# Attention with chunk selection and a gated FFN: eleven SBUF copies as transfers of SyncE, twenty-three loads on Pool's queue, and a new order table

## The chip, the cores and the metric

One core of a Trainium2 chip. The metric is the device time of one execution in microseconds (us). The engines are called as in the profile: PE (TensorE), DVE (VectorE), ACT (ScalarE), POOL (GpSimd) and SP (SyncE, which here issues transfers only). A name such as SPq is the DMA queue that an engine issues into.

## The reference

```python
# q, k, v: (4 batches, 8 heads, 768 tokens, 64), float32
k_min, k_max = k_chunks.min(3), k_chunks.max(3)              # 24 chunks of 32 keys
ub = sum(maximum(q*k_min, q*k_max), -1)                       # a bound per query and chunk
ub = where(causal, ub, -1e9)
top_chunks = argsort(ub)[..., -6:]                            # six chunks for each query
scores = where(selected & causal, q @ k.T / 8, -1e9)
attn_out = softmax(scores) @ v
x = attn_out as (3072 tokens, 512)
out = (sigmoid(x @ w_gate) * (x @ w_val)) @ w_out             # 512 -> 1536 -> 512
```

So each query looks only at the keys of the six chunks with the largest bound, and at none behind itself. All of it is computed by one program.

## The kernel before, in words

*Tiles.* The 24 blocks of 128 tokens are done in eight units u0 to u7 of three blocks, that is 384 columns. u0 takes the first blocks of batches 0, 1 and 2, u1 the blocks 1 to 3 of batch 0, u2 the last two of batch 0 and the first of batch 3, u3 and u4 those of batch 1 with the first free one of batch 2, and so on to u7, the last three of batch 3. A unit's keys and queries are loaded, turned (k and q so that head dimension lies on partitions), their chunk minima and maxima taken (kx), the bounds formed on PE (ub), the six largest chosen (mx), and a mask row per chunk written into the rows that the scores' product reads beside q (ap, apt, hqm). The keys' side holds the turned keys (hk) and the constant pattern of the chunks (hkp).

*Attention.* For each pair of heads PE forms the scores (sc), ACT the exponential (exp), Pool the causal cut where it is needed (cm), PE the product with v (pv), DVE the division (rz, x), and PE turns x back (xps, xT). The first blocks of the batches (u0) run the same steps under names that end in f: vf (load of v), scf, expf, pvf, rzf, xf, xpsf, xTf.

*FFN.* For every unit there are products g and v (gate and value, four matmuls of 128 x 384 each), ACT's tanh, DVE's hg (gate times value) and the product o with w_out, then osb and out. u0 to u3 run this plainly. u4 with u5 and u6 with u7 are done in pairs, by a scheme of seven products for eight (function `ffn_pair`).

*Names.* A number behind the name is the head, pair or half, then the unit or the batch: hk0_2_2 is the even half of batch 2's turned keys for pair 2, hqm1_u5_0 the mask row of u5, k11_2 a quarter of batch 2's k. Batches 1 to 3 load k and q in four transfers each, in runs of 128 bytes; u1 and u2 load theirs by pairs (k0_u1 to q3_u2); v comes by block of 128 tokens (v_2_3), all by SP's queue. The weights wg0 to wo2 come by Pool's queue, converted on the way. Of k, q and v each buffer is used again later, so that a load may have to wait for the last reader of what stood there.

*The order.* All work is entered into a `Plan` with its engines, its reads and its writes. It is then emitted in the order of a long string, `ORDER`, of 1,893 names, written out ahead. In it `name:3` gives the buffer's slot and `name@ACT` an engine other than the first one listed for that operation. Each engine, and each queue, works through its own share of the string in order, so one instruction that waits holds up all behind it on its engine; for a load that waits for its buffer, that is everything behind it on SP.

```python
for op in plan.order():
    op.emit(op.engine)
```

The functions that the change touches, with the lines that the profile names:

Of the kernel before, what the change touches and what calls it, by code (L numbers as in the profile page):

```python
# [94 lines left out]
tri0 ap1 ident epat0:0 ident16 tri k2_u1:0 kn_u1_2:0 kT_u1_2:0 kt_u1_2:0 q1_u2:1 vf1_1:1 epat kcr0 kx0_u1_2  # L95
qn_u2_1@DVE:2 k1_u2 k3_u1 kf1_0:0 q0_u1 qn_u1_0@DVE:3 qT_u1_0:1 qf_u1_0@DVE:0 kx1_u1_2:0 k1_u1 kn_u1_3:4 hkp001@ACT
kT_u1_3:2 q2_u2 hkp010@ACT qf0_0:1 qn_u2_2:5 hkp100@ACT q2_u1 qT_u2_1:3 scm_0:4,5 hkp101@POOL kn_u1_1@POOL:6 kT_u1_1:6
kt_u1_3:1 kx0_u1_3 kx1_u1_1 hq0 hkp000 k0_u1 kn_u1_0@POOL:0 kT_u1_0:7 kt_u1_0@DVE:2 q1_u1 qn_u1_1@POOL:3 qf0_1:2
hq1_u1_0 qf_u2_1:1 hq0_u2_1@POOL qT_u1_1:0 qf1_0 kf0_0 qf_u1_1@DVE q3_u1 kf1_2:3 kfT_0:1 kf16_0@DVE:4 hk0_u1_3@ACT
hk1_u1_3@ACT kx1_u1_3 kx0_u1_1 qfT_0:3 qn_u1_2:2 qf16_0:6 kt_u1_1:1 hk0_u1_2@POOL hkp110@POOL qT_u2_2:0 qn_u1_3@POOL:0  # L100
qT_u1_3:2 qf_u1_3 kn_u2_1:3 vf_1:4 vc_1 qT_u1_2:3 hkf1 hk1_u1_1@POOL hkf0@DVE kx0_u1_0 qm_u1_1:0 kx1_u1_0 kf0_2 qf1_1
kf1_1:5 kfT_2:6 kf0_1 qf0_3:0 qf_u1_2 qm_u1_3@ACT hk0_u1_1@ACT qf1_2:1 qf0_2 hk0_u1_0@POOL vf_2:4 qf_u2_2 vf_0:3 kfT_1:2
kxf1:1 scf_0:1 kf16_2:5 expf_0_0 qfT_1:3 kf16_1@DVE:0 kcr1 kxf0 hkp011 qfT_2:7 scm_1:0,2 qm_u1_0@POOL qf16_1:2 scf_1:2
qm_u1_2@ACT kcr_u1@POOL v10 qf16_2:4 v16_0_0 expf_1_1:3 expf_1_0 hkp111@ACT q3_u2 kcr_f ub_u1:6,4 ubn0_u1:0 ubm0_u1
kf1_3:5 ubn1_u1 k2_u2 qf1_3 pvf_1_1:1 pvf_0_0:3 kT_u2_1:7 mx0_u1:0 pvf_1_0:2 ap0_u1 qfT_3:0 rzf_0_0:0 k0_u2 wg0
hq1_u1_2@POOL wv0 apt0_u1:0 rzf_1_1:1 xf_0_0:0 hk1_u1_0@ACT kn_u2_2:6 qf16_3:0 hq0_u1_1 expf_0_1:1 kT_u2_2:6 kx0_u2_2
hq0_u1_0@POOL vf1_2:2 k3_u2 hq0_u1_2@POOL scm_2:4,0 scf_2:2 expf_2_1:0 hqm0_u1_0 vc_2 xpsf_0_0:5,0 xf_1_1:1 rzf_1_0:0
pvf_0_1:3 rzf_0_1:1 qn_u2_3@POOL:3 xf_1_0:2 q0_u2 sc_u1_0_1:0,1 hqm0_u1_2 expf_2_0 vf1_3:1 xpsf_1_1:1 xTf_1_1 pvf_2_0:4
qn_u2_0:6 xTf_0_0@ACT xpsf_1_0:2 rzf_2_0:0 xTf_1_0 xf_2_0:0 qT_u2_0:5 qf_u2_0@DVE kt_u2_2@DVE:1 kx1_u2_1:0
kn_u2_0@POOL:4 hq0_u1_3@POOL hq1_u1_3@POOL kt_u2_1@DVE:2 hk1_u1_2@POOL qm_u2_1@ACT:0 exp_u1_0_1 sc_u1_1_2:1,3 xpsf_2_0:4  # L110
exp_u1_1_2 xTf_2_0@ACT qT_u2_3:0 qf_u2_3 sc_u1_1_0:2 pvf_2_1:1 rzf_2_1:0 sc_u1_0_0:5 exp_u1_1_0 sc_u1_2_2:4,2 xf_2_1:1
hk1_u2_2@POOL exp_u1_2_2 xf_0_1:2 sc_u1_3_1:0,0 exp_u1_3_1 sc_u1_3_2:2 sc_u1_2_0:4 xpsf_2_1:1 sc_u1_3_0:0 exp_u1_0_0
exp_u1_3_0 v_0_2:2 kf0_3 hk0_u2_2@ACT xTf_2_1 qm_u2_2 ubm1_u1 kx1_u2_2 kn_u2_3@POOL:5 hk0_u2_1@POOL v16_0_2 xpsf_0_1:3
kT_u2_3:5 v_0_3:1 v_0_1:3 wg1 xTf_0_1 sc_u1_0_2:1 ap0 kT_u2_0:0 sc_u1_2_1:6 sc_u1_1_1:3 exp_u1_2_0 exp_u1_1_1 kx0_u2_1
wv1 cm_u1_1 v16_0_1 kx0_u2_0 v16_0_3 exp_u1_2_1 g_u0_0:4,0,0 exp_u1_0_2 tanh_u0_0 kfT_3:7 v_u0_0:3 mx1_u1 kx0_u2_3
ap1_u1 apt1_u1 exp_u1_3_2 kf16_3:6 kt_u2_3@DVE:0 g_u0_1:6,1,1 qm_u2_0@ACT tanh_u0_1 v_u0_1:1 vf_3:0 g_u0_2:4,2,2
v_u0_2:2 hqm1_u1_0@ACT qm_u2_3@ACT hq1_u1_1 pv_u1_1:7 kx1_u2_3 cm_u1_0 pv_u1_0 tanh_u0_2 hq1 sc_u1_4_1:5,3 k11_1:0
hqm1_u1_2 cm_u1_3 exp_u1_4_1 hk1_u2_3@ACT sc_u1_7_0:6,1 g_u0_3:4,3,3 sc_u1_7_2:5 exp_u1_7_0 exp_u1_7_2 wo2 hg_u0_0
hg_u0_1 rz_u1_0:0 x_u1_0:0 kx1_u2_0 cm_u1_2 sc_u1_4_0:3 hg_u0_2 pv_u1_3:1 sc_u1_7_1:7 pv_u1_2 sc_u1_6_2:2,0
sc_u1_5_1:6,2 hq0_u2_3@POOL k01_1 kt_u2_0@DVE:1 rz_u1_1:1 tanh_u0_3 sc_u1_4_2:0 cm_u1_7 kcr_u2@POOL wg2 exp_u1_4_2  # L120
sc_u1_5_2:5 v_u0_3:4 sc_u1_5_0:0 exp_u1_7_1 exp_u1_6_2 exp_u1_5_2 exp_u1_4_0 x_u1_1:1 g_u0_4:1,0,4 sc_u1_6_1:7 ub_u2:2,5
hg_u0_3 xps_u1_0:4,1 ubn0_u2:0 cm_u1_4 wv2 ubn1_u2 mx0_u2:0 ap0_u2 apt0_u2:0 hqm0_u2_2@DVE mx1_u2 pv_u1_4:3 exp_u1_5_0
v_u0_4:0 g_u0_5:2,1,5 wo0 hq0_u2_2@POOL cm_u1_5 vc_3 k00_1 k10_1 hk0_u2_3@ACT exp_u1_6_1 exp_u1_5_1 xT_u1_0@ACT
tanh_u0_4 hg_u0_4 tanh_u0_5 scf_3:7,6,3 pv_u1_7:5 sc_u1_6_0:4 exp_u1_6_0 cm_u1_6 v_u0_5:1 hg_u0_5 g_u0_6:2,2,6 expf_3_0
# [5 lines left out]
pvf_3_1:5 rzf_3_1:1 hg_u0_10 tanh_u0_11 sc_u2_0_2:3,0 o0_u0_0:2,0 exp_u2_0_2 sc_u2_0_1:0 o1_u0_0 hq1_u2_3@POOL  # L130
xTf_3_0@ACT hg_u0_11 xps_u1_3:4 sc_u2_1_0:3 exp_u2_1_0 hqm1_u2_0@ACT hqm1_u2_2@ACT k16_1_0:3 o2_u0_0 o0_u0_1:7,1
xT_u1_3@ACT sc_u2_3_2:6 exp_u2_3_2 o1_u0_1 xf_3_1:0 osb_u0_0@DVE hq1_u2_0@DVE o2_u0_1 hq1_u2_2 hk1_u2_1@POOL osb_u0_1
v_0_4:4 exp_u2_0_1 out_u0_0 xpsf_3_1:3 kx0_1_0 xTf_3_1 cm_u2_1 v16_0_4 sc_u2_1_2:2 sc_u2_0_0:5 exp_u2_0_0 exp_u2_1_2
exp_u2_1_1 o0_u0_2:4,0 o1_u0_2 cm_u2_0 o2_u0_2 g_u1_0:6,3,12 osb_u0_2 tanh_u1_0 v_0_5:2 v16_0_5 cm_u2_2 kx0_1_3
# [158 lines left out]
def kernel(  # L293
# [46 lines left out]
    def copy(e, o, i):  # L340
        if e == ACT:
            nc.scalar.copy(o, i)  # L342
        elif e == DVE:
            nc.vector.tensor_copy(o, i)
        else:
            nc.gpsimd.tensor_copy(o, i)  # L346
# [875 lines left out]
```

## Time and profile before

| | |
|---|---|
| median of three runs | 286.23 us (285.67 to 287.84) |
| the profiled execution | 287.56 us, of which the profile's span is 285.8 |
| PE busy, TensorE weight loads | 268.1 us (94%), 170.8 (60%) |
| DVE, ACT, POOL busy | 230.8 (81%), 213.2 (75%), 120.7 (42%) |
| bytes moved by DMA | 32.69 MB in 123,377 packets, 111,440 of them under 512 B |
| loads of v: issues, size, median from issue to landing | 23, 256 KB, 4.5 us |
| loads of k by blocks | 12, 384 KB, 6.8 us |
| stores of out | 23, 256 KB, 2.1 us |

Times are those of one profiled execution; the 1.76 us between its time and its span lie outside of what the profile shows. In the page's picture of the span every digit is a fortieth of it, 7.1 us. "Idle before" a row is the time for which that engine stood still ahead of it, and the name behind the arrow is what it waited for. A row of the DMA list gives the time from issue to landing.

### The profile page before, as it was taken

What the parts mean: (1) busy time and instruction counts of PE and PEld (TensorE: products, weight loads), DVE (VectorE), ACT (ScalarE), POOL (GpSimd) and SP (SyncE); (2) the same over time, 40 slices, a digit from 0 to 9 for tenths busy, and PEclk for the clock granted to TensorE, in tenths of its full rate; (3) what the DMA queues carried; (4) which work ended last, traced back from release to release, by engine and by line L of the source; (5) the groups of instructions that cost most, each with busy time, mean ns of one, the idle gap of its engine ahead of it and who ended that gap; (6) DMA issues with size and microseconds to landing.
All of it is one profiled execution on the core that took longest, in us unless ns stands there. A gap on an engine that the chain in (4) does not pass through costs nothing.

```text
span 285.8 us, 7062 instructions
## 1 busy us (share of the span) xinstructions
PE 268.1 (94%) x2626; PEld 170.8 (60%) x2626; DVE 230.8 (81%) x626; ACT 213.2 (75%) x452; POOL 120.7 (42%) x199
## 2 busy tenths in 40 slices
PE   1677899999999899999999999999999999999995
...
DMA  6999999999999999998031000100000020100005
GB/s 167 278 225 204 208 209 209 212 174 197 181 214 148 212 214 214 217 181 149 30 85 74 4 2 0 39 37 2 38 3 2 0 110 2 73 37 3 0 17 204
DMA packets 123377, 32.69 MB, mean 114 GB/s; under 512 B 111440, under 2 KB 120400, under 8 KB 123344
## 3 DMA queue, kind: packets, MB, share of 16 engines
...
q8 instruction: 20, 0.33, 0.5%
q14 instruction: 13, 0.11, 0.1%
...
## 4 chain that ended last, share of the span: by engine, by line
PE 74%; DMA 5%; SPq 4%; DVE 3%; ACT 3%; issue 1%; POOL 0%; DVEq 0%
PE o_u L962 19%; PE sc_u L848 10%; PE v_u L931 8%; PE g_u L931 8%; PE pv_u L881 6%; SPq L537 3%; PE sug_u6u L1041 3%; PE suv_u6u L1041 3%; PE sug_u4u L1041 3%; PE suv_u4u L1041 3%; DMA k<-in_k_dram 2%; DMA q<-in_q_dram 2%; PE ube_u L787 2%; PE xps_u L908 1%; PE srv_u6u L1041 1%; PE srg_u6u L1041 1%
## 5 line engine op out<-in xcount | busy, mean ns | idle before, releaser
L859 ACT ACTIVATE att_u<-sc_u 128x512 f16<-128x512 f32 (+3 forms) x184 | 91.4, 556 | 16.2 <-PE sc_u L848 15.0
L962 PE MATMUL o_u<-wo,hg_u 128*128 128x512 f16 x216 | 52.8, 379 | 0.0
L865 POOL TENSOR_SCALAR_AFFINE_SELECT att_u<-att_u 128x384 f16<-128x384 f16 (+1 forms) x56 | 29.1, 529 | 48.7 <-ACT att_u L859 45.8
L931 PE MATMUL v_u<-xT_u,wv 128*128 128x384 f16 x192 | 39.1, 326 | 0.0
L931 PE MATMUL g_u<-xT_u,wg 128*128 128x384 f16 x192 | 39.0, 326 | 0.0
L962 PEld LDWEIGHTS <-hg_u 128*128 128x128 f16 x216 | 20.4, 98 | 20.1 <-issue 0.6
L939 ACT ACTIVATE gate_u<-g_u 128x384 f16<-128x384 f32 x48 | 23.7, 498 | 8.7 <-PE g_u L931 8.5
L943 DVE SCALAR_TENSOR_TENSOR hg_u<-gate_u,v_u 128x384 f16<-128x384 f16 x48 | 25.3, 539 | 5.6 <-PE v_u L931 2.3
L848 PE MATMUL sc_u<-hqe,hke 128*128 128x128 f16 (+2 forms) x220 | 28.7, 243 | 1.2 <-DVE kx_u L561 0.9
L848 PE MATMUL sc_u<-hqo,hko 128*128 128x128 f16 (+2 forms) x220 | 27.6, 243 | 0.5 <-DVE hg_u L943 0.5
L881 PE MATMUL pv_u<-v,att_u 128*128 128x65 f16 x640 | 27.3, 193 | 0.7 <-POOL att_u L865 0.6
L881 PEld LDWEIGHTS <-att_u 128*128 128x128 f16 x640 | 24.7, 98 | 4.9 <-POOL att_u L865 1.1
L931 PEld LDWEIGHTS <-wv 128*128 128x128 f16 x192 | 17.8, 98 | 10.5 <-issue 0.5
L931 PEld LDWEIGHTS <-wg 128*128 128x128 f16 x192 | 18.0, 98 | 10.0
L848 PEld LDWEIGHTS <-hke 128*128 128x128 f16 x220 | 16.7, 98 | 6.8 <-issue 1.6
L848 PEld LDWEIGHTS <-hko 128*128 128x128 f16 x220 | 16.8, 98 | 6.3 <-ACT att_u L859 0.6
L971 ACT ACTIVATE osb_u<-o_u 128x512 f32<-128x512 f32 x17 | 10.1, 606 | 9.3 <-PE o_u L962 9.3
L962 PE MATMUL o_u<-wo,hgp_u 128*128 128x512 f16 (+1 forms) x72 | 17.0, 370 | 0.0
L553 POOL CAST v<-v 128x512 f16<-128x512 f32 x23 | 13.8, 611 | 4.1 <-DMA v<-in_v_dram 3.8
L900 DVE TENSOR_TENSOR x_u<-pv_u,rz_u 128x384 f16<-128x384 f32 (+1 forms) x28 | 14.6, 528 | 0.7 <-PE xps_u L908 0.3
L342 ACT COPY xT_u<-xps_u 128x384 f16<-128x384 f16 (+1 forms) x22 | 10.1, 474 | 5.2 <-PE xps_u L908 5.1
L346 POOL CAST k<-k 128x768 f16<-128x768 f32 x9 | 7.5, 833 | 13.9 <-DMA k<-in_k_dram 13.8
(215 smaller groups left out, 597.3 us busy)
## 6 DMA issues: line engine op xcount, KB each, us to landing
v<-in_v_dram SPq DMA_DIRECT2D x23, 256.0 KB, 4.5
out_dram<-osb_u SPq DMA_DIRECT2D x23, 256.0 KB, 2.1
...
wg<-in_moe_w_gate_dram POOLq DMA_DIRECT2D x3, 512.0 KB, 8.9
wv<-in_moe_w_val_dram POOLq DMA_DIRECT2D x3, 512.0 KB, 10.0
wo<-in_moe_w_out_dram POOLq DMA_DIRECT2D x3, 512.0 KB, 9.1
...
```

What stands on the lines that cost most here:

```text
L342: nc.scalar.copy(o, i)
L553: plan.add(f"v16_{b}_{ib}", {POOL: pool(H * D)}, lambda e: nc.gpsimd.tensor_copy(v16[b % 2][:, ib, :, 0:D], at(t)), reads=[t], writes=[("v ...
L848: nc.tensor.matmul(at(t)[:, o:o + 128 * m], hk[b % 2][e_][:, p, 128 * jb:128 * jb + 128], hq[u.side][e_][:, p, 128 * x:128 * (x + m)], sta ...
L859: plan.add(f"exp_{u.name}_{h}_{y}", {ACT: act(n)}, lambda e, t=t, att=att, b0=b0, n=n: nc.scalar.activation(at(att)[:, b0:b0 + n], at(t), ...
L865: nc.gpsimd.affine_select(out=dv, in_=dv, compare_op=ALU.is_ge, fill=0.0, base=0, pattern=[[0, u.m], [1, 128]], channel_multiplier=-1)
L881: nc.tensor.matmul(at(pv)[:, last, x, :], at(att)[:, c:c + 128], v16[b % 2][:, jb, h, :], start=(jb == 0), stop=(jb == ib))
L900: plan.add(f"x_{u.name}_{p}", {DVE: dve(u.t)}, lambda e: nc.vector.tensor_tensor(at(x_).rearrange("p a (e d) -> p e a d", e=2), at(pv)[:, ...
L931: nc.tensor.matmul(at(t), w16[:, c, 128 * fb:128 * fb + 128], at(u.xt)[:, c, :], start=(c == 0), stop=(c == 3))
L939: plan.add(f"tanh_{u.name}_{fb}", {ACT: act(T)}, lambda e, g=g, gate=gate: nc.scalar.activation(at(gate), at(g), AF.Tanh, scale=0.5), read ...
L943: plan.add(f"hg_{u.name}_{fb}", {DVE: dve(T)}, lambda e, w_=w_, gate=gate, hg=hg: nc.vector.scalar_tensor_tensor(at(hg), at(gate), 1.0, at ...
L962: nc.tensor.matmul(at(o), hgs[c][1][1]()[:, 128 * tb:128 * tb + 128], wo16[:, fc, lo:hi], start=(c == 0), stop=(c == NFB - 1))
L1041: nc.tensor.matmul(at(t), left[i](c), right[i](c), start=first and c == 0, stop=c == 1, skip_group_check=not first)
```

## The change

Four things change in the code, and `ORDER` is a new string throughout.

- `copy`, which picked ACT, DVE or Pool, can now also issue the copy as a transfer inside SBUF on SP's queue.
- A new function `read` issues a load on SP's queue as before, or on Pool's, there with `single_packet=True`.
- The tables of engines of hkp, hkf, hk and hqm have SP as a further choice.
- Those of the loads kf, qf, vf, of u1's and u2's k and q, and of v have POOL as a further choice.

```diff
@@ copy
         elif e == DVE:
             nc.vector.tensor_copy(o, i)
+        elif e == POOL:
+            nc.gpsimd.tensor_copy(o, i)
         else:
-            nc.gpsimd.tensor_copy(o, i)
+            nc.sync.dma_start(o, i)
@@ constants
-                const(f"hkp{i}{e_}{o}", {DVE: dve(2 * S, 4, 64), POOL: pool(2 * S), ACT: act(2 * S, False, 64)},
+                const(f"hkp{i}{e_}{o}", {DVE: dve(2 * S, 4, 64), POOL: pool(2 * S), ACT: act(2 * S, False, 64), SP: (480, 480)},
@@ loads
+    def read(e, o, i):
+        if e == SP:
+            nc.sync.dma_start(o, i)
+        else:
+            nc.gpsimd.dma_start(o, i, single_packet=True)
+
...
-                plan.add(f"{n}f_{b}", {SP: (550, 550)}, lambda e, t=t[n], src=src: nc.sync.dma_start(
+                plan.add(f"{n}f_{b}", {SP: (550, 550), POOL: (930, 930)}, lambda e, t=t[n], src=src: read(e, 
...
-        plan.add(f"v_{b}_{ib}", {SP: (450, 450)}, lambda e: nc.sync.dma_start(
+        plan.add(f"v_{b}_{ib}", {SP: (450, 450), POOL: (930, 930)}, lambda e: read(e, 
@@ the table, around the first weights and the first FFN product: before
-... kT_u2_1:7 mx0_u1:0 pvf_1_0:2 ap0_u1 qfT_3:0 rzf_0_0:0 k0_u2 wg0 hq1_u1_2@POOL wv0 apt0_u1:0 rzf_1_1:1 xf_0_0:0
-... sc_u1_0_2:1 ap0 kT_u2_0:0 sc_u1_2_1:6 sc_u1_1_1:3 ... exp_u1_2_1 g_u0_0:4,0,0 exp_u1_0_2 tanh_u0_0 kfT_3:7 v_u0_0:3
@@ and after
+... qm_u1_2@ACT kn_u2_1:3 v10 wg0 xf_1_0:0 kf0_3 kT_u2_1:4 qm_u1_1@ACT hq1_u1_2 xpsf_1_0:5,0 qf0_3:2 qf1_3 qn_u2_1@DVE:5
+... ubn0_u1:0 xpsf_0_0:1 xpsf_2_0:4 ... xpsf_2_1:6 xTf_2_1 xTf_0_1@ACT g_u0_0:7,0,0 hkp100@ACT tanh_u0_0 hq0_u1_3 v_u0_0:0
```

In the new table these copies go to SP: hkp000 (DVE before), hqm1_u3_2 and hk0_2_3 (ACT), and hk0_2_0, hk0_2_2, hqm1_u5_0, hqm1_u5_2, hk1_3_1, hk0_3_1, hk0_3_2 and hqm1_u7_0 (Pool). These loads go to Pool's queue: q0_u1, q0_u2, q1_u2, q3_u2, kf1_0, kf0_2, qf1_0, vf_2, vf_3 and fourteen of the v blocks. The table was drawn with other figures for transfers in its model than before, so the order of all engines differs: some thirty copies of the pairs' products change between ACT and DVE, and the first loads are now u2's keys, then u1's. The set of PE's products is the same.

More of the change, by code (lines that the diff above doesn't have):

```diff
@@ L94 @@
 ORDER = """
[L95 to L124, printed above, removed]
@@ L130 @@
[L130 to L134, printed above, removed]
@@ new lines @@
+kn_u2_2:2 kT_u2_2:1 k0_u1 kT_u1_1:2 hk1_u2_0 k2_u1 kx1_u2_0:0 kx1_u1_1:1 k3_u1 kf0_0:0 qn_u1_2:3 qT_u1_2:3 epat q3_u1
+kf1_0@POOL vf1_2:4 kt_u2_2@DVE:1 kn_u1_0@POOL:5 q0_u1@POOL hkp110 hk1_u2_2@POOL kx0_u2_2 kt_u1_1@DVE:2 hk0_u2_0@POOL
+kn_u1_2:6 kn_u1_3:0 hkp010@ACT kT_u1_0:4 kx0_u1_0 qf1_1:1 kx0_u2_0 kt_u1_0:0 kx1_u2_2 qn_u1_0@DVE:2 kx1_u1_0 qf_u1_2:0
+qf0_1 kT_u1_2:5 hq1 qfT_1:6 qn_u1_3:1 hk0_u2_2@ACT hkp001@ACT hk0_u1_1@ACT qT_u1_3:7 qf_u1_3 hkp101 kx0_u1_2 kfT_0:0
+qT_u1_0:1 kT_u1_3:3 q2_u2 kf1_2:2 kf1_1:3 kf0_1 kfT_1:4 qf_u1_0@DVE qf16_1:3 kxf0 kx1_u1_2 q1_u1 qf1_0@POOL:4 vf_1:5
@@ new lines @@
+qf0_0 qf1_2:1 kf1_3:0 kf0_2@POOL kfT_2:7 q0_u2@POOL qm_u1_0@ACT:0 hk1_u1_1@ACT scm_1:1,6 kf16_1:5 scf_1:1 q3_u2@POOL
+kt_u1_3:1 expf_1_0 kf16_2:6 hkp111@POOL expf_1_1:2 qm_u1_3@ACT qn_u1_1@POOL:1 hk0_u1_0@POOL vf1_1:2 qT_u1_1:4 vc_1 k1_u2
+q1_u2@POOL kf16_0@DVE:0 kt_u1_2@DVE:2 kx1_u1_3 kx0_u1_1 qn_u2_3@POOL:3 qn_u2_2@POOL:5 vf_2@POOL:3 kx0_u1_3 qf_u1_1
+pvf_1_0:5 qfT_0:1 qT_u2_3:7 qf16_0@DVE:1 pvf_1_1:2 qT_u2_2:6 rzf_1_0:0 scm_0:3,1 scf_0:3 hk1_u1_2@ACT qm_u1_2@ACT
+kn_u2_1:3 v10 wg0 xf_1_0:0 kf0_3 kT_u2_1:4 qm_u1_1@ACT hq1_u1_2 xpsf_1_0:5,0 qf0_3:2 qf1_3 qn_u2_1@DVE:5 rzf_1_1:1
@@ new lines @@
+xf_1_1:1 expf_0_1:1 qf_u2_3:1 xTf_1_0 qf_u2_2@DVE hk1_u1_0@POOL kcr_u1@POOL kxf1:1 wv0 v_0_2@POOL:5 hkp000@SP qf0_2
+qfT_2:2 xpsf_1_1:5 k3_u2 kfT_3:1 hq0 qf16_2@DVE:2 xTf_1_1 kf16_3@DVE:1 hq0_u1_0 kn_u2_3:3 expf_0_0 hk0_u1_2@ACT
+hq1_u1_0@POOL scm_2:6,7 kT_u2_3:0 scf_2:2 vf_0:4 v16_0_0 pvf_0_1:2 kx1_u2_3 pvf_0_0:3 kx0_u2_1 rzf_0_1:0 vc_2@ACT
+expf_2_0 qT_u2_1:5 pvf_2_0:1 expf_2_1:3 qf_u2_1 kcr_f@POOL hk0_u1_3@POOL wg1 xf_0_1:2 rzf_0_0:1 rzf_2_0:0 xf_0_0:0
+kx1_u2_1 xf_2_0:1 wv1 v_0_1@POOL:1 kx0_u2_3 hq0_u1_2 pvf_2_1:6 xpsf_0_1:2 kt_u2_1@DVE:0 rzf_2_1:1 xf_2_1:2 kcr_u2@POOL
@@ new lines @@
+hq0_u1_1 hq0_u2_1 qn_u2_0:3 qfT_3:7 qf16_3:2 kt_u2_3@DVE:2 ub_u1:5,3 qm_u2_1@ACT:0 ubn0_u1:0 xpsf_0_0:1 xpsf_2_0:4
+xTf_0_0@ACT xTf_2_0@ACT xpsf_2_1:6 xTf_2_1 xTf_0_1@ACT g_u0_0:7,0,0 hkp100@ACT tanh_u0_0 hq0_u1_3 v_u0_0:0 v_0_3@POOL:0
+v11 hq1_u2_1@POOL hq1_u1_3@POOL hk1_u1_3@POOL g_u0_1:5,1,1 hkf0 ubm0_u1 mx0_u1:0 ubn1_u1 ap0_u1 ubm1_u1 v_u0_1:1
+g_u0_2:6,2,2 v_u0_2:4 wg2 apt0_u1:0 hqm0_u1_0@DVE sc_u1_0_2:2,1 hg_u0_0 tanh_u0_1 hg_u0_1 hkf1@ACT hqm0_u1_2@ACT
+qm_u2_2@ACT tanh_u0_2 sc_u1_2_0:3,2 sc_u1_3_2:7,3 exp_u1_3_2 exp_u1_0_2 v16_0_2 vf1_3:6 hkp011 sc_u1_3_0:5 exp_u1_3_0
@@ new lines @@
+exp_u1_2_0 qT_u2_0:0 g_u0_3:1,3,3 hg_u0_2 qf_u2_0@DVE tanh_u0_3 sc_u1_2_1:6 exp_u1_2_1 sc_u1_2_2:7 exp_u1_2_2
+sc_u1_0_0:4 hq0_u2_0@DVE v_u0_3:5 sc_u1_1_2:0,0 exp_u1_1_2 sc_u1_1_1:3 exp_u1_1_1 hg_u0_3 mx1_u1 ap1_u1 hq0_u2_3
+hq1_u1_1@POOL cm_u1_3 wo0 g_u0_4:1,0,4 tanh_u0_4 v_u0_4:6 g_u0_5:2,1,5 tanh_u0_5 exp_u1_0_0 hg_u0_4 k10_1:1 k01_1 k00_1
+apt1_u1 wv2 hk0_u2_3@POOL cm_u1_2 v16_0_1 v16_0_3 sc_u1_3_1:5 sc_u1_1_0:7 cm_u1_0 v_u0_5:0 hg_u0_5 sc_u1_0_1:3 hqm1_u1_2
+exp_u1_0_1 ap0 g_u0_6:1,2,6 exp_u1_3_1 exp_u1_1_0 tanh_u0_6 hqm1_u1_0@ACT pv_u1_2:2 v_u0_6:6 pv_u1_3 sc_u1_6_2:4,2
@@ new lines @@
+sc_u3_4_2:2 sc_u3_7_0:0 o0_u1_0:6,1 xps_u3_1:7,1 pv_u3_5:3 exp_u3_4_2 sc_u3_6_1:2 kx0_2_3 o1_u1_0 k16_2_0@ACT:0 hg_u1_11
+rz_u3_0:1 exp_u3_6_1 o2_u1_0 pv_u3_4 x_u3_0:1 exp_u3_7_0 osb_u1_0 o0_u1_1:4,0 xps_u2_3:2 v_3_1:3 exp_u3_6_0 hk0_2_3@SP
+out_u1_0 qf1_u4_2 qf1_u4_1 qf1_u4_0 qm_u4_0@ACT:0 k16_2_1:1 qf1_u4_3 sc_u3_7_1:5 o1_u1_1 kx0_2_1 kx1_2_2 hq1_u4_0@POOL
+hq0_u4_0@POOL cm_u3_6 kt_2_1:5 qm_u4_2@ACT o2_u1_1 hq1_u4_2@ACT xT_u2_3@ACT hk1_2_3@ACT exp_u3_7_1 kt_2_0:6 k00_3:1
+kcr_2@POOL v_2_2:5 hk0_2_0@SP v_1_4@POOL:2 v16_2_5 hq0_u4_2@ACT rz_u3_2:0 x_u3_2:2 ub_u4:0,6 o0_u1_2:1,1 xps_u3_2:2
```

298 lines of the change are left out of this document (152 added, 146 removed).

## The prediction

> **What bounds the kernel now.** I read the page first, for the engine that is busy nearly always.
>
> ```profile
> span 285.8 us, 7062 instructions
> PE 268.1 (94%) x2626; PEld 170.8 (60%) x2626; DVE 230.8 (81%) x626; ACT 213.2 (75%) x452; POOL 120.7 (42%) x199
> PE   1677899999999899999999999999999999999995
> DMA  6999999999999999998031000100000020100005
> ```
>
> TensorE (PE) is busy 94% of the span; only the first five slices and the last are below it by much. The DMA engines are full in slices 2 to 18, the first 130 us or so, and almost empty behind. Then the windows, which say where PE is not fed:
>
> ```profile
> core 0: us, PE busy (x) PEld busy (x) DVE busy (x) ACT busy (x) POOL busy (x), PEclk, DMA share, GB/s
> 0.00:33.00 33.00, 20.06 (x191) 13.80 (x192) 22.30 (x69) 26.64 (x51) 23.96 (x48) 1.00 0.97 218
> 33.00:94.00 61.00, 60.29 (x616) 38.87 (x615) 47.23 (x146) 46.30 (x100) 32.44 (x57) 1.00 1.14 195
> 94.00:281.00 187.00, 186.42 (x1806) 117.20 (x1806) 160.10 (x412) 139.99 (x300) 64.32 (x96) 1.00 0.30 68
> 281.00:286.00 5.00, 1.36 (x17) 0.95 (x14) 1.21 (x2) 0.28 (x1) 0.00 (x0) 0.89 0.49 183
> 90.00:100.00 10.00, 8.82 (x82) 5.24 (x80) 7.85 (x13) 8.26 (x18) 5.53 (x9) 1.00 1.23 206
> ```
>
> Of 33 us at the start PE is idle 12.94; of the 248 us from 33 to 281 it is idle 1.29 in all, 1.18 of it between 90 and 100; the last 5 us are the last block's way out. The granted clock is 1.00 up to there. So there are two ways to change the time. One is the moment at which PE's unbroken run begins and how much of PE's list is already done by then; the other is a new hole in the run. What DVE, ACT and Pool are freed of counts only where PE waits for that very piece. The chain of waits and PE's timeline show the beginning:
>
> ```profile
> 33.00 0.81 PE L931 MATMUL g_u<-xT_u,wg 128*128 128x384 f16 x4
> 33.81 0.44 PE kfT L589 x4
> 34.26 0.82 PE v_u L931 x4
> 35.08 0.65 PE g_u L931 x4
> ```
>
> The first product with a gate weight (g_u0_0) starts at 33.00; the first with a value weight (v_u0_0) at 34.26, and PE runs on from there. And Pool's timeline with the landings of narrow windows of the DMA view:
>
> ```profile
> 21.22 0.61 POOL L553 CAST v<-vf 128x512 f16<-128x512 f32 x1 [1.66 <-DMA vf<-in_v_dram]
> 21.78 0.99 POOL L492 DMA_DIRECT2D wg<-in_moe_w_gate_dram  x1
> 23.27 0.75 POOL L493 DMA_DIRECT2D wv<-in_moe_w_val_dram  x1
> wv<-in_moe_w_val_dram POOLq DMA_DIRECT2D x1, 512.0 KB, 10.9
> ```
>
> wv0 is issued at 23.27 and lands 10.9 later, at 34.2: v_u0_0 begins as its weight lands. The time at which Pool issues wv0 is the first term.
>
> **The change, part by part.** PE's list of products is the same in both kernels, 4702 rows of operands each; what moves is order, engines and queues.
>
> *The start.* In the new order Pool has 26 operations ahead of wv0, before 22. Eight of the new ones are loads (kf1_0, q0_u1, qf1_0, kf0_2, q0_u2, q3_u2, q1_u2, vf_2). No 128 or 256 KB load by Pool is in the trace; the weights' issues are the nearest rows:
>
> ```profile
> L492 POOL DMA_DIRECT2D wg<-in_moe_w_gate_dram x3 | 2.5, 841 | 0.0
> L493 POOL DMA_DIRECT2D wv<-in_moe_w_val_dram x3 | 2.3, 754 | 0.0
> L346 POOL COPY hke<-epat 64x1536 f16<-64x1536 f16 x1 | 1.5, 1457 | 0.1
> 0.00:23.27 23.27, 14.70 (x28) 1.00 0.90 226
> ```
>
> Eight at 0.80 are 6.4 us. Against that, of the two pattern copies of 1.46 ahead of wv0 one is left, and qm_u1_0, hkf1, the first v cast and some keys' and queries' copies of 0.4 to 0.7 move behind it or to other engines. Summed by form, the busy time ahead of wv0 comes to 1.4 us more than the 14.70 of the row. The wait of 1.66 for vf, with its cast, no longer stands ahead of wg0, so the two nearly cancel: I take wv0 at 23.3 again. Bounds: of before's first 23.27 us Pool stood idle 8.57. If a quarter of that is left, wv0 goes out at 16.1 + 2.2 = 18.3; if all of it, at 24.7.
>
> But PE has done less by that moment. The new order has 43 names ahead of v_u0_0, the old 56: twelve groups of u1's scores (36 blocks of 128 columns; 0.65 for the x4 of 384 above is 0.054 each, so 1.94) and qT_u2_0 (two turns of 0.11, from kfT's 0.44 for four: 0.22) come later. The idle time that they filled is lost and the same 2.15 us must be done behind it. **Start: +2.1**, bounds from 18.3 and 24.7 for wv0: −2.9 to +3.6.
>
> *vf_0.* The last of SP's loads of the start is now vf_0, the first block of v of batch 0, and pvf_0_1, which needs it, stands on PE ahead of all that leads to g_u0_0.
>
> ```profile
> 17.81 0.88 SPq L527 DMA_DIRECT2D kq_u<-in_q_dram  x1
> vf<-in_v_dram SPq DMA_DIRECT2D x1, 256.0 KB, 3.8
> v<-in_v_dram SPq DMA_DIRECT2D x1, 256.0 KB, 8.3
> L657 DVE RECIPROCAL rzf<-pvf 128x4 f32<-128x4 f32 x8 | 1.4, 173 | 2.5 <-PE pvf L651 2.4
> L659 DVE TENSOR_TENSOR xf<-pvf,rzf 128x256 f16<-128x256 f32 x8 | 3.2, 410 | 0.1
> ```
>
> From its landing it takes the cast (0.61), pvf (0.3), DVE's list of fourteen pieces to the last turned x (three such reciprocals, four such products, two kx, two kt and the rest: 4.75) and g_u0_0 (0.65): 6.3 us to v_u0_0. It is SP's 28th issue; the 28th of before is the one at 17.81, and a copy (hkp000) and loads that reuse buffers stand ahead of it, so I put it between 17.8 and 22.0, at 20.7. With the 3.8 of the first DMA row it lands at 24.5, and v_u0_0 could start at 30.8, hidden behind wv0. The second row is a load issued beside wg0 at 21.96; issued then, with its 8.3, vf_0 lands at 30.3 and v_u0_0 starts at 36.6, 2.4 late. I take it as hidden, since it is issued before the weights; the other end is a rival.
>
> *The eleven copies.* The pieces taken from the engines are mostly of these forms:
>
> ```profile
> L346 POOL COPY hke<-kt 64x768 f16<-64x768 f16 x10 | 8.4, 841 | 4.8 <-DVE kt L738 4.7
> L346 POOL COPY hqo<-apt_u 64x768 f16<-64x768 f16 x7 | 6.4, 914 | 6.8 <-DVE apt_u L821 3.3 <-DVE rz_u L898 3.3
> L342 ACT COPY hke<-kt 64x768 f16<-64x768 f16 x2 | 1.6, 832 | 0.0
> ```
>
> Eight from Pool, two from ACT, one from DVE: some 9 us of engine time. Pool is 42% and ACT 75% busy while PE waits for neither, so this is worth nothing. What each pays is latency: 0.33 to issue and then the landing. No copy inside SBUF is in the trace; the nearest transfers by SP, alone and under loads, are
>
> ```profile
> out_dram<-osb_u SPq DMA_DIRECT2D x1, 256.0 KB, 2.0
> out_dram<-osb_u SPq DMA_DIRECT2D x1, 256.0 KB, 4.9
> L821 DVE STREAM_TRANSPOSE apt_u<-ap 128x384 f16<-128x384 f16 x8 | 4.5, 568 | 0.2
> L738 DVE STREAM_TRANSPOSE kt<-k 128x768 f16<-128x768 f16 x12 | 11.3, 945 | 0.5 <-POOL k L346 0.5
> 57.93 0.86 PE o_u L962 x4
> ```
>
> so 2.3 to 5.2 against 0.84. Most have many products between source and reader (hkp000, hk0_2_3, hk1_3_1, hk0_3_1, hk0_3_2, hqm1_u7_0); hqm1_u3_2 and hk0_2_0 have some 5 us. Three are tight. hqm1_u5_0: its source apt1_u5 takes 0.57, so 0.57 + 0.33 + 2.0 = 2.9, while PE's list between holds two chains of o (1.73), three score groups and one pv (1.03 by the same 0.054 a block of columns), 2.76 in all: 0.1 late; hqm1_u5_2 comes 0.3 to 0.5 behind it. hk0_2_2, in the loaded part: 0.95 + 0.33 + 2.0 to 4.9 is 3.3 to 6.2 against 3.84 of products, counted the same way: 0 to 2.4 late. **Copies: +1.0** (near the idle row for u5, whose DMA slices show 0 to 1, between the ends for hk0_2_2), bounds 0 and +5.
>
> *The loads of the middle.* Fourteen v blocks and vf_3 leave SP's queue. PE's one hole of the middle:
>
> ```profile
> 92.18 1.84 DVE L561 TRANSPOSE_TENSOR_REDUCE kx<-k 128x24 f32<-128x768 f32 x2 [2.15 <-DMA k<-in_k_dram]
> 94.51 0.32 PE L848 MATMUL sc_u<-hqo,hko 128*128 128x384 f16 x1 [0.53 <-DVE hg_u L943]
> SPq L547 <- POOL hqe L346: 4.4, 1, 4.4
> ```
>
> DVE waits 2.15 for batch 2's k, whose issue SP holds back while it stands at L547, a v load whose buffer is not free (4.4 in one wait). With v on Pool that wait blocks SP no longer, and the hole of 1.18 goes. The bytes stay the same, though, and slices 2 to 18 are full, so loads as a whole come no sooner; batch 2's first reader on PE stands 4.5 us of products earlier than before. **Middle: −1.0**, bounds −1.3 (all of 33 to 281) and +2.
>
> The sum: 287.56 (the profiled execution) + 2.1 + 1.0 − 1.0 = 289.7. The median of the runs is 1.33 below the profiled one, so **288.3**.
>
> **The rivals.** *B, vf_0 behind the weights:* +2.4, 290.7. For it: the load issued beside wg0 took 8.3. Against: vf_0 is expected a microsecond or more ahead of wg0. The Trainium skill ("DMA: Bandwidth & Descriptors", Queues, rings and completion order) states that each DMA engine takes turns between the queues it has work for, a packet at a time; by that a load of SP already under way is slowed too as soon as Pool's queue has packets, which speaks for B. The trace agrees as far as 3.8 became 8.3.
>
> *C, the slower side of the copies:* SP issues in order, and a copy waits on SP for its source, with v, k, q and out behind it; with each landing as under load (4.9, not 2.0) the three tight copies are late: hk0_2_2 by its 2.4, the two of u5 by 0.1 + 2.9 between them, 5.4 in all where 1.0 is in the sum: 288.3 + 4.4 = 292.7. It decides from a landing of about 3 us on. Against: the idle DMA of u5's stretch.
>
> *E, Pool's issue held by DVE:*
>
> ```profile
> L577 DVE TENSOR_SCALAR qm_u<-qf_u 128x256 f32<-128x256 f32 x1 | 1.7, 1698 | 0.0
> L577 DVE TENSOR_SCALAR qm_u<-qf_u 128x320 f32<-128x320 f32 x1 | 0.3, 325 | 0.0
> ```
>
> One qm of DVE, at 30.5, took 1.70 in place of 0.33 while Pool issued wg1 at 31.4: one in Pool's nine issues, 1.37 lost. Over 23 new issues that is 23/9 × 1.37 = 3.5, so 291.8 if all lies on the path; most don't, as PE is behind none of them after 40 us. The Trainium skill ("SBUF — State Buffer", Who interferes with whom) says that DVE and Pool share a port pair as an exclusive lock, and whichever is first blocks the other whole; the row looks like that.
>
> *D, faster:* Pool waits for nothing ahead of wv0 and issues it at 18.3; it lands at 29.2, 5.0 earlier, less the 2.15 of products = −2.9, and with the whole middle hole gone −1.3: 287.56 − 4.2 − 1.33 = 282.0. For it: the wait of 1.66 is gone and the eight loads wait for nothing but buffers. Against: the casts and copies ahead of wv0 still wait for data that comes through full DMA engines, and vf_0's chain then decides at 30.8. *F, it brings nothing:* the loads share the same 16 engines, so only the order counts; that lies inside the forecast.
>
> **How the numbers follow.** Forecast 0.42 (its own range 285.5 to 290.5; 0.34 within 1%, 0.08 above), B 0.15, C 0.11, E 0.06, D 0.26. 1% of 286.23 is 2.9 us, about what a measurement of this kernel can tell from no change: 283.4 to 289.1. Faster is D, 0.26; same 0.34; slower 0.08 + 0.15 + 0.11 + 0.06 = 0.40. The range takes in D and C: 281.5 to 293.5.
>
> **What would show it.** Right: wv0 issued near 23 and v_u0_0 at 34 with no u1 scores ahead of it; no hole at 93; PE waits under 1 us in front of u5's scores. Wrong: wv0 before 20 or after 25; v_u0_0 waiting for x rather than wv; landings of copies over 3 us, or any PE hole over 1 us between 40 and 280 for a key, a mask row or a v block.

## Result, and the profile after

The changed kernel takes 294.0 us (293.23 to 294.85), the kernel before 286.22: 1.0244 times as long, 95% interval 1.0203 to 1.0284. Comparisons leave out executions more than 1.5% above the fastest of the same kernel, so a median given below can lie above what its ratio says. The page of the kernel after, its windows, and the longest wait of PE in it:

```profile
span 292.3 us, 7073 instructions
PE 269.1 (92%) x2626; PEld 172.1 (59%) x2626; DVE 232.2 (79%) x628; ACT 217.4 (74%) x462; POOL 125.3 (43%) x199
PE   2763699999999999999999999999999999999994
```
```profile
0.00:33.00 33.00, 14.95 (x120) 11.07 (x120) 18.92 (x47) 20.18 (x39) 20.23 (x39) 0.92 0.98 225
94.00:281.00 187.00, 186.99 (x1826) 118.09 (x1824) 162.47 (x423) 141.60 (x300) 59.53 (x86) 1.00 0.30 68
```
```profile
PE pvf L660 <- POOL v L562: 6.2, 1, 6.2
```

PE's busy time is nearly what it was (269.1 for 268.1); in the first 33 us it is 14.95 where it was 20.06. From 94 us to 281 PE now has next to no idle time (0.01). One load holds the start: Pool waits for vf (8.5 us), and PE for Pool's cast of it (6.2). Its story in the timelines, with the landing from the DMA view of that instant:

```profile
18.86 0.78 POOL L495 DMA_DIRECT2D wg<-in_moe_w_gate_dram  x1
19.05 0.43 SPq L510 DMA_DIRECT2D vf<-in_v_dram  x1
20.50 0.79 POOL L496 DMA_DIRECT2D wv<-in_moe_w_val_dram  x1
vf<-in_v_dram SPq DMA_DIRECT2D x1, 256.0 KB, 12.1
31.23 0.61 POOL L562 CAST v<-vf 128x512 f16<-128x512 f32 x1 [8.49 <-DMA vf<-in_v_dram]
38.19 0.81 PE L940 MATMUL g_u<-xT_u,wg 128*128 128x384 f16 x4 [0.37 <-ACT xT_u L343]
38.83 0.81 PE L940 MATMUL v_u<-xT_u,wv 128*128 128x384 f16 x4
```

vf_0 goes out 0.2 us behind the first weights and takes 12.1 us, where the same load took 3.8 before. The first value product, v_u0_0, starts at 38.83. It did not wait for its weight, as wv0 landed 10.9 us after its issue, at 31.4.

The profiled execution of before took 1.3 us more than the median of its runs, so that kernel was traced once more (e10_before_again).

> The kernel before, unchanged, for a second trace of it: its profiled execution was 1.3 us above the median of its runs, and the question is where. Expected: 285.3 to 286.3, with the start as it was (v_u0_0 near 34) and the wait of DVE for k of batch 2 near 93 shorter than 2.15 us; if instead the start is the part that varies, v_u0_0 begins near 33.

It took 285.64. The start is all but the same and the hole near 93 is not there:

```profile
span 283.8 us, 7062 instructions
0.00:33.00 33.00, 21.65 (x195) 15.28 (x196) 22.89 (x71) 27.21 (x53) 24.40 (x48) 1.00 1.00 222
34.05 0.82 PE L931 MATMUL v_u<-xT_u,wv 128*128 128x384 f16 x4 [0.48 <-ACT gate_u L939]
90.00:100.00 10.00, 9.99 (x99) 6.04 (x98) 9.76 (x15) 9.67 (x22) 6.71 (x13) 1.00 1.15 221
```

Against this trace the 8.5 us of span (292.3 to 283.8) come apart as: v_u0_0 4.78 later (38.83 to 34.05); 2.15 us of products less done ahead of it, by the count of the prediction (PE's busy time from v_u0_0 on is 248.69 us, 246.33 in the second trace of before, 2.36 more); 0.64 for one wait of PE at 61.5; 0.63 at the end, where the last product is over 3.98 us ahead of the end of the span in place of 3.35. The other 0.3 is spread over the rest.

```profile
61.51 0.30 PE L660 MATMUL pvf<-vf,attf 128*128 128x65 f16 x4 [0.64 <-POOL attf L653]
```

### The profile page after: what moved, and what is told of

Read it like the earlier page. It is cut to its first block, busy times and chain, and to the rows that moved or that the text cites. A ratio compares the mean times of both kernels' runs of the same rounds, so it can differ in the third digit from the quotient of the medians.

```text
span 292.3 us, 7073 instructions
## 1 busy us (share of the span) xinstructions
PE 269.1 (92%) x2626; PEld 172.1 (59%) x2626; DVE 232.2 (79%) x628; ACT 217.4 (74%) x462; POOL 125.3 (43%) x199
## 3 DMA queue, kind: packets, MB, share of 16 engines
q1 hardware_dynamic: 100336, 23.45, 38.1%
## 4 chain that ended last, share of the span: by engine, by line
PE 83%; DMA 8%; ACT 5%; issue 1%; POOL 1%; DVE 1%; SPq 0%; POOLq 0%; ACTq 0%
PE o_u L971 21%; PE sc_u L857 11%; PE v_u L940 9%; PE g_u L940 9%; DMA vf<-in_v_dram 6%; PE pv_u L890 6%; PE ube_u L796 3%; PE sug_u6u L1050 3%; PE sug_u4u L1050 3%; PE suv_u6u L1050 3%; PE suv_u4u L1050 3%; PE xps_u L917 1%; PE srg_u4u L1050 1%; PE srv_u6u L1050 1%; PE srg_u6u L1050 1%; PE srv_u4u L1050 1%
## 5 line engine op out<-in xcount | busy, mean ns | idle before, releaser
L868 ACT ACTIVATE att_u<-sc_u 128x512 f16<-128x512 f32 (+3 forms) x184 | 90.6, 553 | 12.2 <-PE sc_u L857 10.9
L971 PE MATMUL o_u<-wo,hg_u 128*128 128x512 f16 x216 | 53.5, 379 | 0.0
L857 PE MATMUL sc_u<-hqe,hke 128*128 128x128 f16 (+2 forms) x220 | 26.7, 243 | 0.2 <-ACT hqe L343 0.2
L980 ACT ACTIVATE osb_u<-o_u 128x512 f32<-128x512 f32 (+1 forms) x19 | 10.9, 592 | 17.8 <-PE o_u L971 16.3
L819 DVE MAX8 mx_u<-ubn_u 128x8 f32<-128x8 f32 (+16 forms) x152 | 12.7, 159 | 0.3
L512 POOL DMA_DIRECT2D v<-in_v_dram x14 | 12.8, 915 | 0.2 <-issue 0.2
```

What stands on the lines that cost most here:

```text
L512: nc.gpsimd.dma_start(o, i, single_packet=True)
L857: nc.tensor.matmul(at(t)[:, o:o + 128 * m], hk[b % 2][e_][:, p, 128 * jb:128 * jb + 128], hq[u.side][e_][:, p, 128 * x:128 * (x + m)], sta ...
L868: plan.add(f"exp_{u.name}_{h}_{y}", {ACT: act(n)}, lambda e, t=t, att=att, b0=b0, n=n: nc.scalar.activation(at(att)[:, b0:b0 + n], at(t), ...
L971: nc.tensor.matmul(at(o), hgs[c][1][1]()[:, 128 * tb:128 * tb + 128], wo16[:, fc, lo:hi], start=(c == 0), stop=(c == NFB - 1))
```

## The experiments

Theory 1 was that the race between vf_0 and the first weights makes the loss. The rivals: the copies by SP come late for their readers (theory 3), or the new queues and order cost whatever vf_0 does (theory 2). In the tables of order below only the moved names are shown.

**e3_weights_after_vf0**

```diff
-... v10 wg0 xf_1_0:0 ... kxf1:1 wv0 v_0_2@POOL:5 hkp000@SP ... vf_0:4 v16_0_0 pvf_0_1:2
+... v10 xf_1_0:0 ... kxf1:1 hkp000@SP ... vf_0:4 v16_0_0 wg0 wv0 v_0_2@POOL:5 pvf_0_1:2
```

> The changed kernel with wg0, wv0 and v_0_2 moved on Pool from ahead of the cast of vf_0 to right behind it, so that they are issued only when vf_0 has landed. Theory 1 (the weights' transfers make vf_0 late): vf_0, issued near 19, lands in 5 to 6 us instead of 12.1; the weights then go out near 25 and land near 34 and 37, so v_u0_0 starts near 37.5 and the median is 292 to 293.5. Rival (vf_0 is late for the loads ahead of it or for k of batch 1 behind it, not for the weights): it still takes 10 us or more, v_u0_0 starts after 41, and the median is 297 to 299.

290.23 us (289.26 to 292.28), 1.0159 of before (1.0098 to 1.0220). The SP timeline, the DMA view, Pool's timeline and the chain of waits:

```profile
19.20 0.51 SPq L510 DMA_DIRECT2D vf<-in_v_dram  x1
vf<-in_v_dram SPq DMA_DIRECT2D x1, 256.0 KB, 5.1
24.99 0.78 POOL L495 DMA_DIRECT2D wg<-in_moe_w_gate_dram  x1
35.38 1.46 PE v_u L940 x4
```

Same load, same place on SP, issued 0.15 later, the same loads ahead of it and k of batch 1 behind: 5.1 us without the weights, 12.1 with them. So it is what Pool issues just ahead of and behind vf_0: the two weights and v_0_2, which was moved with them. e7, where v_0_2 is on SP's queue, shows below that the weights are enough. Even with both weights held back by six microseconds v_u0_0 starts at 35.38 and the kernel gets faster, by 3.8 us of the medians and 2.4 of the ratios, where 0.5 to 2 was expected.

**e1_vf0_early, e2_copies_back, e5_hkp000_back, e6_ten_copies_back** change by how much vf_0 is ahead of wg0, and what is on SP.

```diff
# e1: vf_0 sooner, in v_0_2's buffer
-... kf0_3 kT_u2_1:4 ... v_0_2@POOL:5 ... scf_2:2 vf_0:4 v16_0_0
+... kf0_3 vf_0:5 kT_u2_1:4 ... v_0_2@POOL:4 ... scf_2:2 v16_0_0
# e5: one copy back on DVE (e2: all eleven back; e6: the ten others)
-... v_0_2@POOL:5 hkp000@SP qf0_2
+... v_0_2@POOL:5 hkp000 qf0_2
```

> The changed kernel with one load moved: vf_0 goes out some 3 us sooner on SP, right behind kf0_3, into the buffer that v_0_2 had, and v_0_2 takes the other. Theory 1 (the loss is vf_0 landing 12.1 us after its issue at 19.05, because it runs beside the weights): vf_0 is issued near 16.2, lands by 21, PE does not wait 6.2 us for its cast, the granted clock stays 1.00, v_u0_0 starts when wv0 lands, near 32 in place of 38.8: the median goes from 294.0 to 288 (286.5 to 290). Theory 2 (the loads and copies on other queues, or the order with less done ahead, cost the time whatever vf_0 does): 292 or more.

> The changed kernel with its eleven copies by SP given back to the engines that had them before; order and loads as changed. Theory 1 (the start alone costs): within 1 us of 294.0, the 0.7 us that hkp000 held SP ahead of vf_0 being the only gain. Theory 3 (transfers inside SBUF come late for their readers, as the prediction priced at 1.0): 1 to 3 us faster, 291 to 293. If the copies' freeing of engines is worth something: slower than 295.

> The changed kernel with only hkp000, the one copy ahead of vf_0 on SP's queue, given back to DVE; the ten other copies stay on SP. Theory 1 (all that the copies cost is the 0.7 us by which hkp000 pushes vf_0's issue past that of wg0): as with all eleven back, vf_0 is issued before 18.8, lands by 24, v_u0_0 starts near 31.7 and the run is at 287.5, or at 292 to 293 in those executions where vf_0 falls behind wg0 all the same; median 287.5 to 290. Theory 3 (the ten others come late for their readers): 292 or more.

> The changed kernel with the ten other copies given back to the engines of before, and hkp000 left on SP. Theory 1: vf_0 still lands 11 to 12 us after its issue, the median is 293 to 295, as the changed kernel. Theory 3 (the ten others are what the eleven gave back): 288 to 291.

Each one's issue of vf_0, issue of wg0 and landing, in the order e1, e2, e5, e6:

```profile
16.49 0.37 SPq L510 DMA_DIRECT2D vf<-in_v_dram  x1
20.12 0.77 POOL L495 DMA_DIRECT2D wg<-in_moe_w_gate_dram  x1
vf<-in_v_dram SPq DMA_DIRECT2D x1, 256.0 KB, 3.4
```
```profile
18.71 0.37 SPq L510 DMA_DIRECT2D vf<-in_v_dram  x1
19.05 0.78 POOL L495 DMA_DIRECT2D wg<-in_moe_w_gate_dram  x1
vf<-in_v_dram SPq DMA_DIRECT2D x1, 256.0 KB, 4.6
23.45 0.61 POOL L562 CAST v<-vf 128x512 f16<-128x512 f32 x1 [0.51 <-DMA vf<-in_v_dram]
30.31 0.81 PE L940 MATMUL g_u<-xT_u,wg 128*128 128x384 f16 x4 [0.63 <-ACT xT_u L343]
```
```profile
18.66 0.37 SPq L510 DMA_DIRECT2D vf<-in_v_dram  x1
18.99 0.78 POOL L495 DMA_DIRECT2D wg<-in_moe_w_gate_dram  x1
vf<-in_v_dram SPq DMA_DIRECT2D x1, 256.0 KB, 7.4
```
```profile
19.28 0.49 SPq L510 DMA_DIRECT2D vf<-in_v_dram  x1
18.95 0.78 POOL L495 DMA_DIRECT2D wg<-in_moe_w_gate_dram  x1
vf<-in_v_dram SPq DMA_DIRECT2D x1, 256.0 KB, 12.9
```

| | issue of vf_0 against wg0 | its landing | time of the traced execution | median (lowest to highest) | ratio to before |
|---|---|---|---|---|---|
| e1 | 3.6 ahead | 3.4 | 288.5 | 291.24 (288.5 to 292.31) | 1.017 (1.0103 to 1.0237) |
| e2 | 0.34 ahead | 4.6 | 287.39 | 289.16 (287.39 to 293.34) | 1.009 (1.005 to 1.013) |
| e5 | 0.33 ahead | 7.4 | 289.53 | 288.46 (286.38 to 290.76) | 1.0071 (1.0032 to 1.0109) |
| e6 | 0.33 behind | 12.9 | 295.87 | 296.48 (291.49 to 298.07) | none |
| changed kernel | 0.19 behind | 12.1 | 293.99 | 294.0 (293.23 to 294.85) | 1.0244 (1.0203 to 1.0284) |

Half a microsecond on either side of wg0 decides over 5 to 8 us of landing. With hkp000 off SP's queue vf_0 goes out 0.34 to 0.39 us sooner (18.71 and 18.66 for 19.05), and that puts it ahead of wg0. Giving back this one copy is worth what all eleven are worth: the intervals of e5 and e2 overlap. e2 itself came out better than its theory 1, which had taken those 0.7 us for a small thing (within 1 us of 294.0). Whether hkp000 costs by its 0.71 us of issue or by its 192 KB, which are under way on SP's queue until 20.7 (17.02 and 3.7), no run separates; in e3 it stands in the same place and vf_0 lands in 5.1. The ten others cost nothing that can be seen. In the changed kernel all ten are issued at 94.83 us or later, and PE is idle for 0.01 us from 94 to 281. So theory 3 is out. e6 itself decides little: its executions spread from 291.49 to 298.07 and give no ratio, and its median lies above the 293 to 295 expected; the landing of 12.9 is what it adds.

e1's traced execution, 288.5, is in the range of theory 1, but it is the shortest of four. The others took 290.7 to 292.31 and were not traced; their mean granted clock was 0.986 to 0.988, that of the traced one 0.999. So e1 fell short of its 288 for a reason that is open. The traced one's chain of waits shows where a risk is left: with vf_0 ahead, k3_u2 is what goes out beside the weights, at 19.52, and lands 6.16 later.

That 287.4 and 293.3 both occur in e2, with a lead of 0.34 us, fits an outcome that differs from execution to execution. The three longest (291.72 to 293.34) had a mean granted clock of 0.982 to 0.987, the seven others 0.991 or more, but none of the three was traced.

**e7_before_vf0_beside_weights**, the race alone, put into the kernel before (the cast v16_0_0 moves along):

```diff
-... vf_2:4 qf_u2_2 vf_0:3 kfT_1:2 ... qf16_2:4 v16_0_0 ... k2_u2 qf1_3 pvf_1_1:1 ... k0_u2 wg0 hq1_u1_2@POOL wv0
+... vf_2:4 qf_u2_2 kfT_1:2 ... qf16_2:4 ... k2_u2 qf1_3 vf_0:3 wg0 wv0 v16_0_0 pvf_1_1:1 ... k0_u2 hq1_u1_2@POOL
```

> The kernel before with three things moved at the start and nothing else: vf_0 on SP from behind vf_2 to behind qf1_3, wg0 and wv0 on Pool from behind the cast of vf_0 to ahead of it. Both are then issued near 20. Theory 1 (a load issued just behind the first weights lands some 12 us later, whatever the rest of the order): vf_0 lands 10 to 12 us after its issue, near 31 instead of 21, v_u0_0 starts 2 to 5 us later than 34.3 and the median is 288.5 to 291.5. Rival (it is the new order's other differences that cost): within 1 us of 286.

292.62 us, 1.0265 of before (1.0209 to 1.0322): as large a loss as the change's, without any of its copies, loads or order, and somewhat more than expected. In the trace v_u0_0 starts at 39.69. But the load that became late was another than I had said. vf_0 was issued level with wg0 and landed in 4.1; q0_u2, behind it, was caught:

```profile
18.98 0.51 SPq L511 DMA_DIRECT2D vf<-in_v_dram  x1
19.00 1.09 POOL L492 DMA_DIRECT2D wg<-in_moe_w_gate_dram  x1
20.68 0.49 SPq L527 DMA_DIRECT2D kq_u<-in_q_dram  x1
kq_u<-in_q_dram SPq DMA_DIRECT2D x1, 128.0 KB, 10.4
31.86 0.69 PE L686 MATMUL qT_u<-ident,qn_u 128*128 128x128 f32 x2 [3.26 <-ACT xT_u L342]
```

In the first trace of before the same load, issued 0.39 us ahead of wg0, took 3.6. The two loads between, k0_u2 and k3_u2, took 7.8 and 8.9 here and 3.9 and 3.7 before. So it isn't something about vf_0: the three small loads that SP issues 0.5 to 1.7 us behind the first weight take 4 to 7 us longer, and the first weights being issued two to three microseconds sooner (19.00 for 21.78) made this kernel slower. The kernel before had late loads too, v_0_2 with 8.3 and kf0_3 with 10.4 behind wg0, but PE had no wait for them.

**e4_v_back_on_sp** (`v_1_3@POOL:5` and thirteen like it become `v_1_3:5`)

> The changed kernel with fourteen of the fifteen loads of v blocks behind the start (all but v_0_2) given back to SP's queue, at the same places of the order. Theory of the prediction's middle part (v on Pool's queue is what removes the hole near 93): a hole of 0.5 to 1.5 us comes back between 60 and 130 us and the median is 294.5 to 295.5. Rival (the new order alone removes it): within 0.5 of 294.0. If Pool's 0.92 us for each of these issues costs anything, it is faster than 293.5.

294.44 us, 1.0311 of before (1.0258 to 1.0365), which overlaps the changed kernel's interval. vf_0 still lands in 11.6. PE's waits behind 40 us:

```profile
PE pv_u L890 <- POOL att_u L874: 0.7, 1, 0.7
PE pv_u L890 <- POOL v L562: 0.2, 1, 0.2
```

A hole of 0.9 came, at 71 us and not near 93; the changed kernel's own hole at 61.5 went. That is what the theory expected as to the hole (0.5 to 1.5 between 60 and 130) and the rival as to the time (within 0.5 of 294.0). Nothing is decided by half a microsecond here: the queue of the v blocks is worth about nothing either way.

**e8_vf0_ahead, e9_both_early, e11_vf3_and_tail**, towards a version without the race:

```diff
# e8
-... v10 wg0 ... kcr_u1@POOL kxf1:1 wv0 v_0_2@POOL:5 hkp000@SP ... k3_u2 kfT_3:1 ... scf_2:2 vf_0:4 v16_0_0
+... v10 ... kcr_u1@POOL wg0 kxf1:1 wv0 v_0_2@POOL:4 hkp000 ... k3_u2 vf_0:5 kfT_3:1 ... scf_2:2 v16_0_0
# e9, against e8
-... kf0_3 kT_u2_1:4 ... wv0 v_0_2@POOL:4 hkp000 ... k3_u2 vf_0:5 ... wv1 v_0_1@POOL:1
+... kf0_3 vf_0:5 kT_u2_1:4 ... wv0 hkp000 ... k3_u2 ... wv1 v_0_2@POOL:4 v_0_1@POOL:1
# e11, against e8
-... hqm1_u1_2 ... cm_u1_7 vf_3@POOL:3 ... o2_u6_1 o1_u7_0 o1_u6_2 o2_u6_2 o2_u6_0 osb_u6_0 out_u6_0 osb_u6_1 out_u6_1
+... hqm1_u1_2 vf_3@POOL:3 ... cm_u1_7 ... o2_u6_1 osb_u6_1 out_u6_1 o1_u7_0 o1_u6_2 o2_u6_2 osb_u6_2 out_u6_2 o2_u6_0 osb_u6_0 out_u6_0
```

> The changed kernel with hkp000 on DVE, vf_0 in the buffer that v_0_2 had and right behind k3_u2 on SP, and wg0 behind kcr_u1 on Pool, a microsecond later: vf_0 goes out near 17.8, two microseconds ahead of wg0, in every execution. Theory 1: it lands by 23, the granted clock is 1.00 in all runs, v_u0_0 starts near 31.7 to 32.5, and the median is 286.8 to 288 with little spread. If something else besides that race holds the start: 289 or more, or runs at 292 remain. It beats the kernel before only if the middle's 1 us is worth more than the 2.15 us of scores that are left for later: 285.5 at best.

286.9 us (285.93 to 289.29), 1.0051 of before (1.0023 to 1.0080). vf_0 is 1.6 us ahead of wg0 and lands in 5.3; v_u0_0 starts at 31.76:

```profile
18.34 0.41 SPq L510 DMA_DIRECT2D vf<-in_v_dram  x1
19.95 0.78 POOL L495 DMA_DIRECT2D wg<-in_moe_w_gate_dram  x1
vf<-in_v_dram SPq DMA_DIRECT2D x1, 256.0 KB, 5.3
31.76 0.81 PE L940 MATMUL v_u<-xT_u,wv 128*128 128x384 f16 x4
54.53 0.30 PE L660 MATMUL pvf<-vf,attf 128*128 128x65 f16 x4 [0.74 <-POOL attf L653]
```

That is 2.3 sooner than in the second trace of before and, less the 2.15 of scores left over, level. Most of the loss is back, with the order and the loads of the change all but unchanged, so theory 2 is out as the main cause. The granted clock was not 1.00 in all runs, as expected, but 0.986 to 1.000. What is left in the trace is the wait at 54 (vf_3, issued by Pool at 46.58, lands 6.6 later) and the bunched stores at the end. Two ways on from here:

> The changed kernel with hkp000 on DVE, vf_0 right behind kf0_3 on SP in the buffer that v_0_2 had, wg0 behind kcr_u1 on Pool, and v_0_2 behind wv1 on Pool in place of behind wv0. Theory 1 (what counts is which transfers are under way when the weights start, and then the landing of wv0): vf_0 lands near 20, k3_u2 by 23, wv0, with 256 KB less beside it, by 30, so v_u0_0 starts at 29.5 to 30.5, and the median is 284.8 to 286.0, below the 286.9 with vf_0 behind k3_u2 and about level with the kernel before or just under it. If v_0_2 is now late for its cast, a hole of 1 us or more shows up between 40 and 50 and the median is 287 or more.

288.69 us (288.09 to 289.27), 1.0083 of before (1.0055 to 1.0110): a miss, by the second branch. PE's waits behind 40 us:

```profile
PE pvf L660 <- POOL attf L653: 1.3, 1, 1.3
PE pv_u L890 <- POOL v L562: 0.8, 2, 0.6
```

v_0_2 is late for its cast, vf_3 later still, and wg0 went out at 21.29, so that wv0 landed no sooner (at 31.9, in e8 at 31.2).

> The version with vf_0 two microseconds ahead of wg0 (286.9), with the two other places where its trace is behind a typical trace of the kernel before: vf_3 goes out on Pool some 3 us sooner, behind hqm1_u1_2, so that its landing no longer makes PE wait 0.74 us for the cut of u0's second part of batch 3 near 54; and the stores of u6's second and third block stand right behind their products, where the changed order had them bunched with those of u7 (the last landing came 2.9 us after PE's end, 2.25 in the kernel before). Theory 1 with these two as all that is left: 285.4 to 286.2, level with the kernel before. If the rest of the difference lies elsewhere: 286.6 or more.

285.28 us (284.4 to 286.54), 0.9983 of before (0.9962 to 1.0004): level with the kernel before, with ten copies and all 23 loads still on the queues that the change gave them, and with the changed order but for these few names. No wait of PE between 40 us and 280 is left that the view would list. So a few names make up the whole loss: e8's, which end the race, and the load vf_3 with the order of the last stores. These last two were moved together, so what each is worth is not shown.

## Why the prediction was right and wrong

*Right: the bound, and the sign with luck.* PE's start decides, and v_u0_0 had 2.15 us fewer products ahead of it, as counted: no u1 scores are there before it. The size is not right: the forecast was 2.1 us above 286.23, the measured loss is 7.8. 294.0 lies half a microsecond past the top of the range, 293.5 (by the ratio, 1.0244 times 286.23, it is 293.2), and that top was set by C, which did not happen. Slower had the largest chance, 0.40, only as the sum of four cases; the forecast alone, 288.3, was within what passes for no change. Two of the signs of being wrong came: v_u0_0 waited for x, not for wv, and five of the eleven copies took over 3 us to land.

*Wrong: the forecast's step "I take it as hidden".* It hung on vf_0 being issued well ahead of the weights. I had vf_0 at 20.7 and the weights as before, wg0 at 21.8 and wv0 at 23.3; vf_0 came at 19.05 and wg0 at 18.86. Pool stood idle less than I took: wv0 went out at 20.50, between my 23.3 and the bound of 18.3. Its busy time ahead of wv0 was well counted (16.27 for 16.1), its idle time was 4.2 us where the 23.3 holds 7.2. So what rival D saw (Pool gets there early) came true in part, and did the opposite of what D priced: it started the race that B described. The two were written down as separate cases with separate chances; they are one, since an earlier wg0 is a later vf_0.

*Wrong: B's price.* B took the 8.3 us of one load beside wg0; the load took 12.1, and from the start of its cast to g_u0_0 it is 6.96 (31.23 to 38.19) where I had 5.65 from the landing on. I had that stretch run over DVE's list; in the trace its chain runs over PE from 31.89 to 37.16, at a granted clock of 0.50. So the start came to 4.8 + 2.15 = 6.9, not 2.1, and not B's 4.5. B's mechanism stands, as e3 and e7 show. The Trainium skill ("DMA: Bandwidth & Descriptors", Queues, rings and completion order) has the engines take turns between queues by packets. A load of SP's that takes 12.1 us beside the weights and 5.1 without them agrees with it. For an estimate, the rows of the profile page of before, where Pool's queue (q0) carries the weights alone:

```profile
q1 hardware_dynamic: 118448, 27.47, 45.3%
q0 software_dynamic: 4752, 4.72, 10.2%
```

A packet of Pool's queue carries 4.72 MB / 4752 = 0.99 KB and one of q1, with SP's loads, 0.23 KB. If these are the packets by which turns are taken, equal turns give the weights some 4 times the bytes. No run here shows that, nor separates turns from other ways of sharing.

*Wrong: copies at +1.0.* The ten behind the start cost 0: PE is idle for 0.01 us from 94 to 281, where all of them are. They landed about as the two rows of the price had it, in 2.1 to 5.4 us for 2.0 to 4.9, but PE waited for none. The first row below is that of the five copies of keys' even halves, the second that of hkp000:

```profile
hke<-kt SPq DMA_DIRECT2D x5, 96.0 KB, 3.9
hke<-epat SPq DMA_DIRECT2D x1, 192.0 KB, 3.7
```

What I had not priced is the one whose landing I had rightly called harmless. I had hkp000 ahead of vf_0 on SP, as part of the 20.7, but not what the third of a microsecond by which it holds vf_0 back decides.

*Wrong: the middle at −1.0.* The second trace of before does not have the hole near 93. I took it off as a gain, and then took off 1.33 for the same execution being above the median: one thing counted twice. In that second execution, near the median, there was nothing to gain.

*E and C did not happen*: no PE wait goes back to a copy by SP, and Pool's 14 v loads took 915 ns each to issue, with nobody waiting for that.
